# Blocks of 512 tokens in tile order behind one block of 192, in place of 26 blocks of 480

## Chip, core and metric

The kernel runs on one core of a Trainium2 chip. The metric is the device time of one execution in microseconds (us); the time shown is the median of three runs. The core's engines are TensorE (PE in the rows, its weight loads PEld), VectorE (DVE), ScalarE (ACT), GpSimd (POOL) and SyncE (SP, which issues the DMAs).

## What is computed

12480 tokens of 128 channels go through an attention with 32 inducing points and then through two feed-forward layers of width 2048. All inputs are float32 or float64; the output is float32.

```python
def mab(q, kv):
    s = scale * (q @ kv.transpose(0, 2, 1))
    s = s - s.max(-1, keepdims=True)
    a = np.exp(s)
    a /= a.sum(-1, keepdims=True) + 1e-09
    return a @ kv
h = mab(I, x)                                # 32 inducing points attend to all tokens
x = mab(x, h)                                # each token attends to the 32 rows of h
x = (s * np.maximum(x @ w_in, 0)**2 + b) @ w_out                       # layer 1
x = f(x @ w_in2) @ w_out2       # layer 2; f(h) = h if h>=1, 0 if h<=-1, else (h+1)**2/4
```

## The kernel before, in words

**Tiling.** The tokens are cut into `NB` = 26 blocks of `TB` = 480 = `TP` x `KB` = 120 partitions x 4 tokens (lines 21 to 25). A block is loaded with four consecutive tokens on each partition, turned by four TensorE transposes, and copied from PSUM to `xT[bl]` with a strided write that restores the order of the tokens (`transposes`, line 240). For the layers a block is the moving operand of every matmul, 480 columns wide; the inner width 2048 is 16 chunks of 128, two chunks to a step, so a block takes `SPB` = 8 steps and the kernel 208 steps for each layer.

**Attention.** In groups of four blocks: `scores` (each block's 32 rows side by side in one PSUM bank), a running maximum, the exponential, and `weighted`, which sums tokens into `hsum`. `finish` makes `hT`, 128 columns wide. Beside it the float64 weights of both layers are loaded as pairs of 32-bit words and converted to float32 (`convert`, line 369), in 16 pieces of 512 columns; the last pieces are those of layer 2.

**First block.** `first_soft` makes the layer-1 input `qt[0]` of block 0 by a way of its own (`f_st` to `f_qt`, lines 770 to 799). The other blocks go in groups of four through `soft_scores` to `soft_move`, and one by one through `soft_q` and `soft_split`. 26 blocks make groups of 1, 4, 4, 4, 4, 4, 4 and 1.

**A step.** Step t does layer 1 of step t and layer 2 of step t - `LAG`, with `LAG` = 13. Layer 1: `in1` has 2 matmuls on float32r operands, `relu1` and `sq1` run on ScalarE, `split1` on GpSimd, and `out1` has one float32 matmul, which the trace shows as two records, and 3 float32r ones. Layer 2: `in2` has 6 float32r matmuls, `clip2`, `g2` and `split2_lo` run on VectorE, `sq2` on ScalarE, `split2_hi` in turns on ScalarE and GpSimd, `out2` has 6 float32r matmuls, and after 8 steps `store` turns the block and writes it with four DMAs. In all, 17 float32r matmuls and one float32 matmul to a step; all of them take new weights.

**The ramp.** Before step 13 only layer 1 runs (`ramp_step`, line 865), beside the conversions, and its `out1_whole` uses two float32 matmuls to a step. Layer 2 can begin its element-wise work only when `close` has given the conversions' space to it, after the last conversion.

**Order.** Each engine runs its instructions in the order in which they were written out. For the attention, the ramp and the last 13 layer-2 steps, a small planner (`Plan`, line 83) places every operation by modelled costs and the list `JOBS` or `TJOBS`, and `best` takes the engine on which an operation would end first; between them the order within a step is the string `ORDER`.

```python
def in1(t):
    nc.tensor.matmul(p[:, j, :TB], hw[f // 4][:, ...], qt[bl], start=True, stop=True)
def out1(t):
    nc.tensor.matmul(p, wo_w[:, f0, :], g[:, 0, :], start=(f0 == 0), stop=False)      # float32
    nc.tensor.matmul(p, wo_hi[:, f1, :], hi[:, 0, :], start=False, stop=False)        # float32r
```

Of the kernel before, what the change touches and what calls it, by code (L numbers as in the profile page):

```python
# [17 lines left out]
C = 128  # L18
NM = 32
DFF = 2048  # L20
TP = 120
KB = 4
TB = TP * KB
NB = 26
NQ = TB // NM
GB = 4
# [23 lines left out]
T1 = 201  # L50
# [25 lines left out]
i195 i196 h194 u206 u207 v c195 c196 l194 i197 g195 i198 g196 c197 g197 s195 o193 c198 i199 o194  # L76
g198 i200 o195 s196 c199 i201 o196 g199 c200 s198 g200 c201 s197 i202 c202 o197 i203 s200 g202 o198
g201 s199 c203 i204 g203 s201 o199 s202 i205 o200 s203 c204 i206 c205 o201 o202 g205 s205 o203 g204
c206 i207 s204 g206 s206 c207 o204 o205 o206 g207 s207 o207
"""  # L80

# [56 lines left out]
def moe_attn_kernel(ctx: ExitStack, tc: tile.TileContext, x, ind, w_in, w_out, s, b, w_in2, w_out2, out):  # L138
# [10 lines left out]
    xT = [kt([C, TB], f"xT{i}") for i in range(NB)]  # L149
# [71 lines left out]
    def blocks(g):  # L221
        return range(min(GB, NB - g * GB))

    def load_x(g, *deps):
        def one_block(i):
            if i == 0:
                xc[g] = pre.tile([TP, GB * KB, C], F32, tag="xc", name=f"xc{g}", bufs=XB)
            t0 = (g * GB + i) * TB
            nc.sync.dma_start(out=xc[g][:, i * KB:(i + 1) * KB, :],
                              in_=x[0][t0:t0 + TB].rearrange("(p k) c -> p k c", k=KB))  # L230

        for i in blocks(g):
            xd[g, i] = dma(0.69, lambda i=i: one_block(i), *deps, at=g * XPACE)
# [5 lines left out]
    def transposes(g):  # L239
        for i in blocks(g):  # L240
            bl = g * GB + i

            def on_pe(i=i, bl=bl):
                T["tr", bl] = ptile("tr", f"ptr{bl}", TRB)
                for k in range(KB):
                    nc.tensor.transpose(T["tr", bl][:, k * TP:(k + 1) * TP], xc[g][:, i * KB + k, :], ident[:TP, :TP])

            def evac(eng, bl=bl):
# [3 lines left out]
            t = add("PE", 0.8 if g == 0 else 0.41, on_pe, xd[g, i], P.get(("xT", bl - TRB)))  # L252
            P["tr", bl] = t
            P["xT", bl] = best(tuple(c for c in (("ACT", 0.45), ("DVE", 0.57)) if c[0] in EVAC), evac, t)

    def scores(g):
        nb = len(blocks(g))
        n = NM * nb

        def on_pe():  # L260
            ps = T["sc", g] = ptile("sc", f"psc{g}", 2)
            for i in blocks(g):
                nc.tensor.matmul(ps[NM * i:NM * (i + 1), :TB], iT, xT[g * GB + i], start=True, stop=True)

        def top():
            ps, old = T["sc", g], T.get(("m", g - 1))
            m = T["m", g] = small("m", g)
            if g == 0:
                nc.vector.reduce_max(m, ps[:, :TB], axis=AX.X)
            else:  # L270
                mx = small("mx", g)
                nc.vector.reduce_max(mx[:n], ps[:n, :TB], axis=AX.X)
# [6 lines left out]
        def expo():  # L279
# [3 lines left out]
            nc.scalar.activation(e[:n], ps[:n, :TB], AF.Exp, bias=nm[:n], scale=scale, accum_out=l[:n])  # L283
# [8 lines left out]
        xs = [P["xT", g * GB + i] for i in blocks(g)]  # L292
# [6 lines left out]
    def weighted(g):  # L299
        nb = len(blocks(g))  # L300
        n = NM * nb

        def tr():
            pe = T["pe", g] = pp.tile([128, KB, 128], F32, tag="pe", name=f"pe{g}", bufs=1)
            e = T.pop(("e", g))[:n].rearrange("n (p k) -> n k p", k=KB)
            for k in range(KB):
                nc.tensor.transpose(pe[:TP, k, :n], e[:, k, :], ident[:n, :n])

        def evac(eng):
            eT = T["eT", g] = pre.tile([TP, KB, 128], F32, tag="eT", name=f"eT{g}", bufs=3)  # L310
            copy(eng, eT[:, :, :n], T.pop(("pe", g))[:TP, :, :n])

        def on_pe():
            ph, eT = ptile("ph", f"ph{g}", 1), T.pop(("eT", g))
            T["ph", g] = ph
            for k in range(KB):
                for i in blocks(g):
                    nc.tensor.matmul(ph[NM * i:NM * (i + 1), :C], eT[:, k, NM * i:NM * (i + 1)],
                                     xc[g][:, i * KB + k, :], start=(k == 0), stop=(k == KB - 1))
# [191 lines left out]
    def finish():  # L511
        t = add("PE", 0.12, f_pm, P["top", NG - 1], P["xT", NB - 1])
# [106 lines left out]
    def step_tile(tag, t, bufs, dt=F32):  # L619
        p = pool["wk" if tag in ("g1", "hi1", "lo1") else "wk2"]  # L620
        return p.tile([128, 1 if tag in ("hi1", "lo1") else GW, TB], dt, tag=tag, name=f"{tag}_{t}", bufs=bufs)

    def relu1(t):
        g = step_tile("g1", t, G1B)
        nc.scalar.activation(g, h1.pop(t)[:, :, :TB], AF.Relu)  # L625
        g1[t] = g
# [19 lines left out]
    def outp(t, hi, lo, whi, wlo, acc, nm, js=range(GW)):  # L646
# [4 lines left out]
        p = acc[bl][:, :TB]  # L651
# [7 lines left out]
    def y1_of(t):  # L659
# [3 lines left out]
        return y1p[bl][:, :TB]  # L663
# [17 lines left out]
    def evac1(bl):  # L681
        y1f[bl] = wtile([128, TB], "y1f", f"y1f{bl}", 1)
        nc.scalar.activation(y1f[bl], y1p.pop(bl)[:, :TB], AF.Identity, bias=bcol, scale=s_sb)

    def evac1_hi(bl, eng="Pool"):
        y1h[bl] = wtile([128, TB], "y1h", f"y1h{bl}", YB, F32R)
        copy(eng, y1h[bl], y1f[bl])

    def evac1_lo(bl, eng="Pool"):
        y1l[bl] = wtile([128, TB], "y1l", f"y1l{bl}", YB, F32R)  # L690
# [5 lines left out]
    def in2(t, js=range(GW)):  # L696
# [42 lines left out]
    def store(bl):  # L739
        o = pool["wk2"].tile([128, NQ, NM], F32, tag="o", name=f"o{bl}", bufs=2)  # L740
# [29 lines left out]
    def f_st():  # L770
        ps = T["st"] = mbank("st_0")
        for k in range(KB):
            nc.tensor.matmul(ps[:TP, 0, k * NM:(k + 1) * NM], xT[0].rearrange("c (p k) -> c k p", k=KB)[:, k, :],
                             hT[:, :NM], start=True, stop=True)

    def f_se():
        e = sm[0, "e"] = wtile([128, NQ, NM], "se", "se0")[:TP, :KB, :]
        nc.vector.tensor_copy(e, T.pop("st")[:TP, 0, :KB * NM].rearrange("p (k j) -> p k j", j=NM))
# [3 lines left out]
    def f_sd():  # L782
        soft_sum(0)
        soft_mul(0, "DVE")
        a2 = T["a2"] = wtile([TP, KB, 2, 2, NM], "qin", "a2", GB)
        eb = sm[0, "e"].unsqueeze(2).to_broadcast([TP, KB, 2, NM])
# [3 lines left out]
    def f_sq():  # L790
        ps = T["qt"] = bank("qt_0")
        for k in range(KB):
            nc.tensor.transpose(ps[:, 0, k * TP:(k + 1) * TP],
                                T["a2"][:, k].rearrange("p h r j -> p (h r j)"), ident[:TP, :TP])

    def f_qt():
        q = qt[0] = wtile([128, TB], "qt", "qt0", 2, F32R)
        nc.vector.tensor_copy(q.rearrange("c (p k) -> c k p", k=KB),
                              T.pop("qt")[:, 0, :TB].rearrange("c (k p) -> c k p", k=KB))
# [6 lines left out]
    def first_soft():  # L806
        t = P["st"] = add("PE", 0.42, f_st, P["hT"])
        t = add("DVE", 0.6, f_se, t)
        left["h2"].append(t)
        t = add("ACT", 0.21, lambda: soft_e(0), t)  # L810
# [314 lines left out]
```

## Time and profile before

| | |
|---|---|
| time, median of 3 runs | 1056.59 us (1055.17 to 1060.0) |
| the profiled execution's own time | 1055.07 us |
| its span, first to last instruction | 1053.3 us |
| PE busy | 1014.7 us, 96% of the span |
| DVE busy | 841.9 us, 80% |
| ACT busy | 787.3 us, 75% |
| POOL busy | 664.2 us, 63% |

A row of the timeline gives start, time taken, engine, line, operation, the tile written and those read, shapes, and in square brackets the idle time before it and what ended it. Matmuls overlap, so the cost of one in a dense stretch is the distance from its start to the next one's start, not its duration. In the table of stretches, each engine's busy time stands with its number of instructions, and PEclk is TensorE's granted clock as a share of 2.4 GHz.

### The profile page before, as it was taken

What the parts mean: (1) busy time and instruction counts of PE and PEld (TensorE: products, weight loads), DVE (VectorE), ACT (ScalarE), POOL (GpSimd) and SP (SyncE); (2) the same over time, 40 slices, a digit from 0 to 9 for tenths busy, and PEclk for the clock granted to TensorE, in tenths of its full rate; (3) what the DMA queues carried; (4) which work ended last, traced back from release to release, by engine and by line L of the source; (5) the groups of instructions that cost most, each with busy time, mean ns of one, the idle gap of its engine ahead of it and who ended that gap; (6) DMA issues with size and microseconds to landing.
All of it is one profiled execution on the core that took longest, in us unless ns stands there. A gap on an engine that the chain in (4) does not pass through costs nothing.

```text
span 1053.3 us, 12315 instructions
## 1 busy us (share of the span) xinstructions
PE 1014.7 (96%) x4445; PEld 777.8 (74%) x4445; DVE 841.9 (80%) x850; ACT 787.3 (75%) x842; POOL 664.2 (63%) x680
## 2 busy tenths in 40 slices
PE   6886899999999999999999999999999999999997
PEld 4553577777777777777777777777777777777775
DVE  4899978877887778788777887877887778877776
ACT  6747478778787777787777777777877777877754
POOL 3757657665567656576656666565766656665565
PEclk9988899999999999999999999999999999999999
DMA  8712001100001000011000010000020000000001
GB/s 260 225 43 76 1 0 27 31 7 4 10 10 38 10 10 10 1 19 38 1 10 10 10 33 15 10 8 3 13 44 1 10 10 10 10 11 10 0 10 20
DMA packets 65668, 28.13 MB, mean 27 GB/s; under 512 B 54135, under 2 KB 61463, under 8 KB 65607
## 3 DMA queue, kind: packets, MB, share of 16 engines
q1 hardware_dynamic: 65606, 27.35, 11.3%
q8 instruction: 35, 0.57, 0.2%
q14 instruction: 27, 0.21, 0.1%
HBM read 14.80 MB, written 6.39 MB: 20 GB/s over the span
## 4 chain that ended last, share of the span: by engine, by line
PE 87%; DVE 7%; ACT 1%; issue 1%; POOL 1%; SPq 0%; DMA 0%; DVEq 0%; ACTq 0%; POOLq 0%
PE y L669 15%; PE y L655 8%; PE y L656 8%; PE h L704 8%; PE y L657 8%; PE h L706 8%; PE h L705 8%; PE h L615 8%; PE y L671 4%; PE y L672 4%; PE y L670 4%; DVE cva_out L404 1%; PE s L550 1%; DVE cva_out L408 1%; DVE cvs_out L401 0%
## 5 line engine op out<-in xcount | busy, mean ns | idle before, releaser
L711 DVE TENSOR_SCALAR cl<-h 128x960 f32<-128x960 f32 (+1 forms) x210 | 239.7, 1143 | 106.8 <-PE h L706 105.4
L182 POOL TENSOR_SCALAR hi<-g 128x480 fp32r<-128x480 f32 x195 | 132.9, 682 | 298.4 <-PE y L672 294.9
L625 ACT ACTIVATE g<-h 128x960 f32<-128x960 f32 x208 | 202.4, 973 | 146.2 <-PE h L615 141.3
L733 DVE TENSOR_TENSOR lo<-oo,hi 128x960 fp32r<-128x960 f32 x196 | 243.7, 1243 | 69.0 <-ACT hi L178 54.8
L715 ACT ACTIVATE cl<-cl,mhalf 128x960 f32<-128x960 f32 (+1 forms) x210 | 228.5, 1090 | 73.0 <-DVE cl L711 73.0
L640 POOL TENSOR_TENSOR lo<-g,hi 128x480 fp32r<-128x480 f32 x195 | 240.3, 1232 | 16.3
L720 DVE SCALAR_TENSOR_TENSOR oo<-h,cl 128x960 f32<-128x960 f32 (+1 forms) x210 | 238.0, 1136 | 7.8 <-ACT cl L715 4.4
L630 ACT ACTIVATE g<-g 128x960 f32<-128x960 f32 x206 | 207.5, 1008 | 5.7
L669 PE MATMUL y<-g,wo_w 128*128 128x480 f32 x390 | 188.6, 565 | 0.0
L704 PE MATMUL h<-y1h,wi_hi 128*128 128x480 f32 x416 | 159.3, 383 | 5.0 <-DVE oo L720 5.0
L655 PE MATMUL y<-hi,wo_hi 128*128 128x480 f32 x416 | 159.3, 383 | 0.6 <-ACT hi L178 0.6
L706 PE MATMUL h<-y1l,wi_hi 128*128 128x480 f32 x416 | 159.0, 382 | 0.0
L705 PE MATMUL h<-y1h,wi_lo 128*128 128x480 f32 x416 | 158.8, 382 | 0.0
L657 PE MATMUL y<-hi,wo_lo 128*128 128x480 f32 x416 | 158.0, 380 | 0.0
L656 PE MATMUL y<-lo,wo_hi 128*128 128x480 f32 x402 | 153.7, 382 | 0.8 <-DVE lo L733 0.7
L670 PE MATMUL y<-hi,wo_hi 128*128 128x480 f32 x195 | 146.6, 752 | 0.6 <-POOL hi L182 0.6
L615 PE MATMUL h<-qt,hw 128*128 128x480 f32 x416 | 127.4, 389 | 1.8 <-ACT g L625 1.1
L178 ACT CAST hi<-oo 128x960 fp32r<-128x960 f32 (+1 forms) x110 | 105.9, 966 | 3.8 <-DVE oo L720 2.1
L182 POOL TENSOR_SCALAR hi<-oo 128x960 fp32r<-128x960 f32 x100 | 100.6, 1006 | 2.9 <-DVE oo L720 2.9
L655 PEld LDWEIGHTS y<-hi,wo_hi 128*128 128x128 f32 x416 | 78.2, 188 | 19.0 <-POOL lo L640 4.7
L615 PEld LDWEIGHTS h<-qt,hw 128*128 128x128 f32 x416 | 78.3, 189 | 18.8 <-issue 2.5
L704 PEld LDWEIGHTS h<-y1h,wi_hi 128*128 128x128 f32 x416 | 78.2, 188 | 18.4 <-DVE oo L720 3.7
(146 smaller groups left out, 1216.4 us busy)
## 6 DMA issues: line engine op xcount, KB each, us to landing
xc<-in_x_dram SPq DMA_DIRECT2D x26, 240.0 KB, 6.1
out_dram<-o SPq DMA_DIRECT2D x104, 60.0 KB, 2.0
qin<-se SPq DMA_DIRECT2D x100, 60.0 KB, 2.0
raw_in<-in_moe_w_in_dram SPq DMA_DIRECT2D x8, 512.0 KB, 6.0
raw_out<-in_moe_w_out_dram SPq DMA_DIRECT2D x8, 512.0 KB, 6.1
ind_sb<-in_inducing_dram SPq DMA_DIRECT2D x1, 16.0 KB, 6.5
s_sb<-in_moe_s_dram SPq DMA_DIRECT2D x1, 0.5 KB, 6.2
b_sb<-in_moe_b_dram SPq DMA_DIRECT2D x1, 0.5 KB, 6.0
```

Source lines behind the costliest of these rows:

```text
L615: nc.tensor.matmul(p[:, j, :TB], hw[f // 4][:, (f % 4) * 128:(f % 4 + 1) * 128], qt[bl], start=True, stop=True)
L640: engine[eng].tensor_sub(lo1[t], g1[t][:, 1:], hi1[t].bitcast(F32))
L655: nc.tensor.matmul(p, whi[:, f, :], hi[:, j, :], start=first, stop=False)
L656: nc.tensor.matmul(p, whi[:, f, :], lo[:, j, :], start=False, stop=False)
L657: nc.tensor.matmul(p, wlo[:, f, :], hi[:, j, :], start=False, stop=last)
L669: nc.tensor.matmul(p, wo_w[:, f0, :], g[:, 0, :], start=(f0 == 0), stop=False)
L704: nc.tensor.matmul(p[:, j, :TB], wi2_hi[:, fs], y1h[bl], start=True, stop=False)
L705: nc.tensor.matmul(p[:, j, :TB], wi2_lo[:, fs], y1h[bl], start=False, stop=False)
L706: nc.tensor.matmul(p[:, j, :TB], wi2_hi[:, fs], y1l[bl], start=False, stop=True)
L711: nc.vector.tensor_scalar(cl[t][:, part(js)], h2[t][:, part(js), :TB], -1.0, 1.0, op0=ALU.max, op1=ALU.min)
L720: nc.vector.scalar_tensor_tensor(oo[t][:, part(js)], h2[t][:, part(js), :TB], -1.0, cl[t][:, part(js)], op0=ALU.max, op1=ALU.add)
L733: engine[eng].tensor_sub(lo2[t][:, part(js)], oo[t][:, part(js)], hi2[t][:, part(js)].bitcast(F32))
```

## The change

Blocks have 512 tokens (128 partitions x 4), and there are 25: block 0 has 192 tokens (96 partitions x 2), the other 24 have 512. Every matmul, element-wise operation and tile of a block takes its width from `tb(bl)`. The tokens of a block stay in the order of its tiles (column k x 128 + p is the token on partition p, place k) from the transposes to the output; `store` puts the order right in the address pattern of its DMAs. The copies out of PSUM in `transposes` and `f_qt`, and the reads of `e` in `weighted`, are contiguous thereby. The attention takes blocks 1 to 24 in six groups of four and block 0 last by itself. There are 200 steps in place of 208, `LAG` stays 13, the end's list `TJOBS` is the same list with every number 8 lower, and the groups of the second attention are 1 and six times 4. The planner's costs of ScalarE, VectorE and GpSimd operations are scaled with the block (`us`). The diff, cut to its core:

```diff
-TP = 120
+TP = 128
 KB = 4
 TB = TP * KB
-NB = 26
+TP0, KB0 = 96, 2
+TB0 = TP0 * KB0
+NB = 25
...
-T1 = 201
+T1 = 193
...
+def tokens(bl):
+    if bl:
+        return TP, KB, TB, TB0 + (bl - 1) * TB
+    return TP0, KB0, TB0, 0
+def tb(bl):
+    return TB if bl else TB0
+def us(d, bl):
+    return 0.06 + (d - 0.06) * tb(bl) / 480
...
     def blocks(g):
-        return range(min(GB, NB - g * GB))
+        return list(enumerate(range(g * GB + 1, (g + 1) * GB + 1) if g < NG - 1 else [0]))
...
             def evac(eng, bl=bl, n=n):
-                copy(eng, xT[bl].rearrange("c (p k) -> c k p", k=KB),
-                     T.pop(("tr", bl))[:, :TB].rearrange("c (k p) -> c k p", k=KB))
+                copy(eng, xT[bl], T.pop(("tr", bl))[:, :n])
...
-            nc.tensor.matmul(p[:, j, :TB], hw[f // 4][:, (f % 4) * 128:(f % 4 + 1) * 128], qt[bl],
+            nc.tensor.matmul(p[:, j, :tb(bl)], hw[f // 4][:, (f % 4) * 128:(f % 4 + 1) * 128], qt[bl],
                              start=True, stop=True)
...
-        p = acc[bl][:, :TB]
+        p = acc[bl][:, :tb(bl)]
...
-        nc.vector.transpose(o.rearrange("p q d -> p (q d)"), y2p.pop(bl)[:, :TB])
-        ov = out[bl * TB:(bl + 1) * TB].rearrange("(q t) (r d) -> r t q d", t=NM, d=NM)
+        nc.vector.transpose(o.rearrange("p q d -> p (q d)"), y2p.pop(bl)[:, :n])
+        ov = out[t0:t0 + n].rearrange("(q t k) (r d) -> r t k q d", t=NM, k=kb, d=NM)
         for r in range(C // NM):
-            nc.sync.dma_start(out=ov[r], in_=o[NM * r:NM * (r + 1)])
+            nc.sync.dma_start(out=ov[r], in_=o[NM * r:NM * (r + 1)].rearrange("p (k q) d -> p k q d", k=kb))
...
-        for k in range(KB):
-            nc.tensor.matmul(ps[:TP, 0, k * NM:(k + 1) * NM], xT[0].rearrange("c (p k) -> c k p", k=KB)[:, k, :],
+        for k in range(KB0):
+            nc.tensor.matmul(ps[:TP0, 0, k * NM:(k + 1) * NM], xT[0][:, k * TP0:(k + 1) * TP0],
                              hT[:, :NM], start=True, stop=True)
...
-        a2 = T["a2"] = wtile([TP, KB, 2, 2, NM], "qin", "a2", GB)
+        a2 = T["a2"] = wtile([TP0, KB0, 2, 2, NM], "qin", "a2", GB)
...
-        nc.vector.tensor_copy(q.rearrange("c (p k) -> c k p", k=KB),
-                              T.pop("qt")[:, 0, :TB].rearrange("c (k p) -> c k p", k=KB))
+        nc.vector.tensor_copy(q, T.pop("qt")[:, 0, :TB0])
...
-        sq = best((("ACT", 0.89), ("DVE", 1.07), ("Pool", 2.17)), lambda e: sq1(a, e), t, bias=SQB)
+        sq = best((("ACT", us(0.95, bl)), ("DVE", us(1.07, bl)), ("Pool", us(2.17, bl))), lambda e: sq1(a, e), t, bias=SQB)
```

## Rows read from the trace of the kernel before

**Rows 1.** Table of stretches: start and end, length, busy times, clock, DMA, GB/s.
```profile
60.00:70.00 10.00, 7.81 (x23) 4.49 (x23) 9.07 (x16) 1.70 (x4) 7.26 (x8) 0.67 0.20 52
...
100.00:110.00 10.00, 6.08 (x10) 2.83 (x11) 9.86 (x12) 0.46 (x1) 7.40 (x6) 0.59 0.00 0
...
120.00:130.00 10.00, 6.72 (x21) 5.43 (x20) 9.20 (x9) 6.87 (x7) 5.38 (x5) 0.66 0.01 2
...
200.00:400.00 200.00, 200.00 (x846) 157.17 (x845) 158.87 (x148) 156.38 (x162) 126.59 (x135) 1.00 0.07 13
...
600.00:800.00 200.00, 200.00 (x845) 157.16 (x844) 160.66 (x152) 156.87 (x163) 128.73 (x135) 1.00 0.09 18
```

**Rows 2.** Chain that ended last, in order of time (start, us, what): steady steps.
```profile
146.46 0.81 PE y L669 x2
150.98 0.81 PE y L669 x2
...
868.43 0.92 PE s L550 x2
```

**Rows 3.** Timeline of PE at full clock, 703 to 705 us.
```profile
703.12 0.38 PE L704 MATMUL h<-y1h,wi_hi 128*128 128x480 f32 x1
...
704.88 0.38 PE L657 MATMUL y<-hi,wo_lo 128*128 128x480 f32 x1
```

**Rows 4.** Timeline of PE at half clock, 126 to 127 us.
```profile
126.11 0.60 PE L655 MATMUL y<-hi,wo_hi 128*128 128x480 f32 x1
126.51 0.60 PE L656 MATMUL y<-lo,wo_hi 128*128 128x480 f32 x1
```

**Rows 5.** Timeline of PEld: weight loads for matmuls of one column.
```profile
63.87 0.86 PEld L843 LDWEIGHTS bsum<-b_sb,wo_s 128*128 128x128 f32 x7 [0.40 <-issue]
```

**Rows 6.** Timeline of DVE in the ramp.
```profile
62.35 0.96 DVE L575 TENSOR_SCALAR mx<-mx 120x4 f32<-120x4 f32 x1
...
63.55 1.22 DVE L580 TENSOR_TENSOR se<-se,mx 120x128 f32<-120x128 f32 x1
64.80 0.67 DVE L787 CAST a<-se 120x256 fp32r<-120x256 f32 x1
65.51 1.45 DVE L788 TENSOR_TENSOR a<-se,a 120x256 f32<-120x256 f32 x1
...
68.00 1.01 DVE L798 CAST qt<-qt 128x480 fp32r<-128x480 f32 x1 [0.33 <-PE qt L793]
...
71.58 1.16 DVE L632 TENSOR_TENSOR g<-g 128x960 f32<-128x960 f32 x1 [0.44 <-ACT g L625]
...
101.65 2.22 DVE L632 TENSOR_TENSOR g<-g 128x960 f32<-128x960 f32 x1
```

**Rows 7.** ACT's copies out of PSUM, grouped by form.
```profile
L178 ACT COPY xT<-ptr 128x480 f32<-128x480 f32 x26 | 25.1, 1095 | 8.0 <-PE ptr L246 8.0
...
L178 ACT COPY eT<-pe 120x512 f32<-120x512 f32 x6 | 3.9, 654 | 0.0
```

**Rows 8.** Timeline of all engines, 13 to 18 us.
```profile
13.71 3.66 ACT L178 COPY xT<-ptr 128x480 f32<-128x480 f32 x4 [2.89 <-PE ptr L246]
...
17.84 0.43 DVE L401 TENSOR_SCALAR cvs_in<-cvs_in 128x512 f32<-128x512 f32 x1 [4.28 <-ACT cvs_in L387]
```

**Rows 9.** Chain that ended last, where layer 2 begins.
```profile
118.48 1.57 DVE wo_lo L427
120.04 1.08 DVE cl L711
...
121.20 1.10 ACT cl L715
...
122.33 1.17 DVE oo L720
...
123.54 0.77 PE h L704
```

**Rows 10.** Chain that ended last, near the end.
```profile
1020.52 2.26 POOL lo L733
...
1041.73 1.17 DVE lo L733
```

More of the change, by code (lines that the diff above doesn't have):

```diff
@@ L20 @@
 DFF = 2048
-TP = 120
+TP = 128
 KB = 4
 TB = TP * KB
-NB = 26
+TP0, KB0 = 96, 2
+TB0 = TP0 * KB0
+NB = 25
 NQ = TB // NM
+NQ0 = TB0 // NM
 GB = 4
@@ L148, in moe_attn_kernel @@
     ident = kt([128, 128], "ident")
-    xT = [kt([C, TB], f"xT{i}") for i in range(NB)]
+    xT = [kt([C, tb(i)], f"xT{i}") for i in range(NB)]
     wo_w = kt([128, WH, C], "wo_w")
@@ L221, in blocks, with one_block @@
     def blocks(g):
-        return range(min(GB, NB - g * GB))
+        return list(enumerate(range(g * GB + 1, (g + 1) * GB + 1) if g < NG - 1 else [0]))
     def load_x(g, *deps):
-        def one_block(i):
+        def one_block(i, bl):
             if i == 0:
                 xc[g] = pre.tile([TP, GB * KB, C], F32, tag="xc", name=f"xc{g}", bufs=XB)
[L228 to L233, printed above, removed]
+            tp, kb, n, t0 = tokens(bl)
+            nc.sync.dma_start(out=xc[g][:tp, i * KB:i * KB + kb, :],
+                              in_=x[0][t0:t0 + n].rearrange("(p k) c -> p k c", k=kb))
+        for i, bl in blocks(g):
+            xd[g, i] = dma(us(0.69, bl), lambda i=i, bl=bl: one_block(i, bl), *deps, at=g * XPACE)
     def dma(dur, fn, *deps, at=0.0):
@@ L258, in scores @@
         n = NM * nb
+        cols = tb(blocks(g)[0][1])
         def on_pe():
             ps = T["sc", g] = ptile("sc", f"psc{g}", 2)
-            for i in blocks(g):
-                nc.tensor.matmul(ps[NM * i:NM * (i + 1), :TB], iT, xT[g * GB + i], start=True, stop=True)
+            for i, bl in blocks(g):
+                nc.tensor.matmul(ps[NM * i:NM * (i + 1), :cols], iT, xT[bl], start=True, stop=True)
         def top():
@@ L290, in total @@
                                            op0=ALU.mult, op1=ALU.add)
-        xs = [P["xT", g * GB + i] for i in blocks(g)]
+        xs = [P["xT", bl] for _, bl in blocks(g)]
         P["sc", g] = add("PE", 0.22 * nb, on_pe, *xs, P["iT"], P.get(("ex", g - 2)), P.get(("sc", g - 1)))
@@ L301, in weighted @@
         n = NM * nb
+        tp, kb, _, _ = tokens(blocks(g)[0][1])
         def tr():
             pe = T["pe", g] = pp.tile([128, KB, 128], F32, tag="pe", name=f"pe{g}", bufs=1)
-            e = T.pop(("e", g))[:n].rearrange("n (p k) -> n k p", k=KB)
-            for k in range(KB):
-                nc.tensor.transpose(pe[:TP, k, :n], e[:, k, :], ident[:n, :n])
+            e = T.pop(("e", g))
+            for k in range(kb):
+                nc.tensor.transpose(pe[:tp, k, :n], e[:n, k * tp:(k + 1) * tp], ident[:n, :n])
         def evac(eng):
             eT = T["eT", g] = pre.tile([TP, KB, 128], F32, tag="eT", name=f"eT{g}", bufs=3)
-            copy(eng, eT[:, :, :n], T.pop(("pe", g))[:TP, :, :n])
+            copy(eng, eT[:tp, :kb, :n], T.pop(("pe", g))[:tp, :kb, :n])
         def on_pe():
@@ L315, in on_pe @@
             T["ph", g] = ph
[L316 to L319, printed above, removed]
+            for k in range(kb):
+                for i, _ in blocks(g):
+                    nc.tensor.matmul(ph[NM * i:NM * (i + 1), :C], eT[:tp, k, NM * i:NM * (i + 1)],
+                                     xc[g][:tp, i * KB + k, :], start=(k == 0), stop=(k == kb - 1))
         def total():
```

121 lines of the change are left out of this document (62 added, 59 removed).

## Prediction

> **What bounds the kernel now.** I read the table of stretches first. From 130 us to near the end TensorE has no idle time at all and the full clock, while VectorE and ScalarE are busy for about 80% [rows 1]: there the time is the sum of the matmuls. Before 130 us it is otherwise. VectorE is busy for 91 to 99% of the ramp's stretches while TensorE waits, partly at half clock [rows 1]; the chain of waits runs along VectorE's conversions of weights up to 120.04 us, and only then layer 2 starts [rows 9]. So the change has two accounts: what TensorE must still do after the ramp, and when the ramp ends.
>
> Next, the price of a matmul. In the chain a step starts every 4.52 us, and its float32 matmul (two records) takes 0.81 us [rows 2]; the other 17, float32r, take (4.52 - 0.81) / 17 = 0.218 us. The timeline agrees: eight distances in 1.76 us are 0.220 us each [rows 3]. At 2.4 columns per ns 480 columns are 0.200 us, so about 0.018 us are over. At half clock the distance is 0.40 us, which is 480 columns at 1.2 GHz with nothing over [rows 4]. The float32 matmul passes its columns four times, 0.800 us at full clock, with 0.01 over. What the 0.018 us are decides this change, and since every float32r matmul after the ramp has 480 columns the trace can't show it directly:
> - a fixed cost of each matmul: 512 columns take 0.2133 + 0.018 = 0.2313 us;
> - a lower rate for float32r: 0.218 x 512 / 480 = 0.2325 us;
> - a floor that the columns don't set: 0.218 us still (a rival, below).
> Weight loads in front of matmuls of one column follow each other at (0.86 - 0.19) / 6 = 0.112 us [rows 5] (0.19 us is the duration of a single load), so a load alone is no floor of 0.218 us. I take 0.232 us, between the first two, which differ little.
>
> The Trainium skill, page "TensorE: Matmul & The Clock Gate", section "Back-to-back issue gap", gives a warm distance of N / 2.4 + 2.5 ns, so 202.5 ns for 480 columns and 215.8 ns for 512. The trace disagrees: 218 ns at 480. If the excess over that rule were only a floor, its 215.8 ns would fit below 218 ns, and the sum would be that of the floor rival.
>
> **The matmuls after the ramp.** Before: layer 1 has 208 - 13 = 195 steps with 2 + 3 float32r matmuls and one float32; layer 2 has 208 steps with 12. That is 975 + 2496 = 3471 float32r x 0.218 + 195 x 0.81 = 756.7 + 158.0 = 914.7 us. After: layer 1 has 200 - 13 = 187 steps, all at 512 columns; layer 2 has 192 steps at 512 and 8 at 192. That is 935 + 2304 = 3239 x 0.232 = 751.4 us; 96 narrow matmuls; 187 x 0.81 x 512 / 480 = 187 x 0.864 = 161.6 us. A narrow matmul streams for 0.08 us, less than a weight load, so I take the load's 0.112 us [rows 5], 10.8 us in all; its bounds are 0.098 us (0.08 + 0.018) and 0.324 us (the float32 matmul's 0.81 x 192 / 480). The sum is 923.8 us: +9.1 us. It grows although 128 matmuls fewer run in 8 steps fewer, because 13 steps of the ramp now cover 8 x 192 + 5 x 512 = 4096 token-steps of layer 1 in place of 13 x 480 = 6240. The 2144 missing ones come later. A step of 512 takes 17 x 0.232 + 0.864 = 4.81 us; 4.52 x 512 / 480 is 4.82 us: wider blocks alone bring next to nothing. With 0.2313 us the sum is 2.3 us less, with 0.2325 us 1.6 us more.
>
> **The ramp.** What is gained must come here, and VectorE sets its end, so I count VectorE's work.
> - First block's softmax: the sum's TENSOR_SCALAR, the multiplication, the two steps of `a2` and the copy to `qt` take 0.96 + 1.22 + 0.67 + 1.45 + 1.01 = 5.31 us [rows 6]. The last four halve or better (128 and 256 elements to a partition become 64 and 128; the copy goes from 480 to 192 and is now contiguous); the 0.96 us were spent on four elements and may stay. I take -2.4 us (-1 to -3.5).
> - Squares of layer 1 that the planner gave to VectorE: 1.16 and 2.22 us [rows 6]. The first is of block 0 and falls to about 0.5 us; the second, of block 1, grows to 2.36 us or goes to ScalarE, which block 0's narrow steps leave freer. I take -1.5 us (+0.1 to -3.4).
> - `xT` copies: strided, 1095 ns; a contiguous copy of 512 columns from PSUM is 654 ns [rows 7]. That frees ScalarE some 24 x 0.44 = 10 us, but ScalarE sets no end later. It matters at 13.7 us, where four copies run for 3.66 us and VectorE waits 4.28 us for the square queued behind them [rows 8]. Four times about 0.35 us is 1.4 us; I take -1.3 us (0 to -1.4, zero if a DMA was the later one).
> - The attention's last group, 192 columns in place of 480: one maximum and one exponential shorter, -0.6 us. The output part of layer 1 for block 0 is smaller, -0.35 us; the groups of the second attention are wider, +0.3 us.
> Together -5.9 us, from +1 to -9 with the order of the queues left open: a planner places all of it anew, and the same conversions on VectorE take twice as long in some places as in others.
>
> At layer 2's start `clip2`, `sq2` and `g2` of the first step run one after another from 120.04 to 123.50 us before TensorE goes on [rows 9]. With 384 in place of 960 elements they take about half: -1.8 us (0 to -2).
>
> **The rest.** One group of the second attention is gone: -0.9 us, its matmuls in the chain [rows 2]. At the end, between 1017 and 1043 us, the chain passes 14 operations of VectorE, ScalarE and GpSimd, 13.7 us in all, such as 2.26 and 1.17 us [rows 10]; 6.7% more columns make +0.9 us. The store's DMAs move the same bytes in as many pieces of 128 bytes, beside other work but for the last: 0, at most +0.5 us. In the steady steps all engines' operations grow with TensorE's step, so none becomes the bound: 0. In the eight narrow steps TensorE has 5 x 0.232 + 0.864 + 12 x 0.112 = 3.37 us, and ScalarE, which in a full step has 156.38 / 200 of 4.81 us [rows 1], 3.76 us, has less than that with layer 2 narrow: 0, at most +0.4 us to a step, 3 us.
>
> **The sum.** +9.1 - 5.9 - 1.8 - 0.9 + 0.9 = +1.4 us. The profiled execution took 1055.1 us (a span of 1053.3 us and 1.8 us around it), so it would be 1056.5 us; it lies 1.5 us below the median, so by the median 1058 us. With the bounds of each term the forecast reaches from 1050 to 1065 us.
>
> **Rivals.**
> - *The float32r distance is a floor.* If weight load and hand-over make the 0.218 us, 512 columns (0.2133 us) fit under it. Then 3335 x 0.218 + 161.6 = 888.6 us, 26.1 us less than now; with the other terms (-7.7 us) the median is 1023 us. For it: the half-clock distance has nothing over [rows 4], as under a floor. Against: loads alone come every 0.112 us [rows 5]. Chance 0.10.
> - *Columns and weights share a read rate.* 480 + 128 columns in 0.218 us are 2789 per us; 512 + 128 take 0.2295 us, and the narrow ones 0.115 us. The matmuls come to 916.0 us, +1.3 us, and the median to 1050 us. The lack of any excess at half clock and in float32 fits this too. Chance 0.12.
> - *The ramp gives more:* every VectorE term at its good end, the median at 1050 to 1052 us. Chance 0.10.
> - *The narrow block is dear (slower).* Place: steps 13 to 20, 96 matmuls of layer 2. If they cost 0.218 us each, that is +10.2 us, 1068 us; at the float32 price of 0.324 us +20.4 us, 1078 us. It decides from about 0.16 us on, where it adds 4 us to the forecast. For it: no float32r matmul of under 480 columns is in the trace. Against: one-column matmuls run at the load's 0.112 us [rows 5]. Chance 0.15.
> - *The ramp doesn't shrink:* VectorE's conversions only fill the freed time with waits for GpSimd. Then the matmuls' +9.1 us stay, less a little: 1064 us. Chance 0.08.
>
> **How the numbers follow.** The forecast has 0.45. A measurement of this kernel tells about 0.5%, 5.3 us, from no change, so "same" is 1051.3 to 1061.9 us. Faster: the floor 0.10, the shared rate 0.10 of 0.12, the larger ramp gain 0.08 of 0.10, and 0.04 of the forecast: 0.32. Slower: 0.12 of the narrow block, 0.07 of the ramp that doesn't shrink and 0.09 of the forecast: 0.28. The rest, 0.40, is the same. The range 1043 to 1069 us leaves out the floor (0.10) and the dearer half of the narrow block (0.07).
>
> **What would show it.** In the profile after: the distance of float32r matmuls at 512 columns (0.231 to 0.233 us forecast, 0.218 us floor, 0.2295 us shared) and a step of 4.81 us; that of the narrow ones in layer 2's first eight steps (0.112 us); the last conversion's end on VectorE about 6 us before 120 us and TensorE going on 1.7 us after it; TensorE without idle time between. I am wrong most if the distance at 512 columns is near 0.218 us or that at 192 columns is not near 0.11 us.

## The result, and the profile after

The changed kernel takes 1065.7 us (median of 5 runs, 1065.04 to 1066.77) against 1056.59 us: ratio 1.008, interval 1.0057 to 1.0103. It is slower by 9 us, 0.7 us beyond the upper end of the forecast (1065 us), though inside the range. The profiled execution took 1066.77 us with a span of 1065.0 us; that of the kernel before had 1053.3 us.

The table of stretches after, with the columns of [rows 1]:

```profile
60.00:70.00 10.00, 6.96 (x34) 5.90 (x34) 8.94 (x19) 2.65 (x5) 8.12 (x8) 0.80 0.17 53
...
100.00:110.00 10.00, 4.63 (x8) 1.89 (x7) 9.83 (x12) 5.92 (x7) 6.50 (x6) 0.75 0.00 0
...
120.00:130.00 10.00, 8.36 (x37) 6.16 (x36) 7.50 (x13) 7.70 (x11) 6.72 (x6) 0.83 0.01 2
...
200.00:400.00 200.00, 200.00 (x793) 147.28 (x791) 158.24 (x140) 154.36 (x152) 123.74 (x125) 1.00 0.07 12
```

The picture is the old one: from 140 us to about 1030 us TensorE has no idle time and the full clock; from 60 to 120 us VectorE is busy for 87 to 98% of every 10 us while TensorE waits. So the two accounts of the prediction can be read separately. The chain of waits gives the point where they meet (start, us, what):

```profile
121.81 0.48 DVE cl L734
...
122.31 0.62 ACT cl L738
...
122.95 0.57 DVE oo L743
```

and TensorE's timeline shows where it goes on:

```profile
123.57 0.36 PE L727 MATMUL h<-y1h,wi_hi 128*128 128x192 f32 x1 [1.53 <-DVE oo L743]
```

The last conversion ends at 121.81 us, 1.8 us later than before [rows 9] instead of 6 us earlier. `clip2`, `sq2` and `g2` then take 1.71 us to the end of `oo` in place of 3.46 us, and TensorE goes on at 123.57 us, against 123.54 us before [rows 9]. So in this execution the ramp brought nothing at all. From there to the end of the span it is 1065.0 - 123.57 = 941.4 us in place of 1053.3 - 123.54 = 929.8 us: +11.7 us, where the prediction had +9.1 us.

The matmuls behind that, on TensorE's timeline, first wide, then narrow ones (compare [rows 3]):

```profile
702.80 0.39 PE L728 MATMUL h<-y1h,wi_lo 128*128 128x512 f32 x1
...
705.14 0.40 PE L680 MATMUL y<-hi,wo_lo 128*128 128x512 f32 x1
```

```profile
139.40 0.27 PE L728 MATMUL h<-y1h,wi_lo 128*128 128x192 f32 x1
...
140.51 0.27 PE L680 MATMUL y<-hi,wo_lo 128*128 128x192 f32 x1
```

Ten wide distances in 2.34 us are 0.234 us each (0.2334 us is the mean over the dense part), ten narrow ones in 1.11 us are 0.111 us each. A steady step takes 4.82 us, which is 4.52 x 512 / 480; without its 17 x 0.2334 us, 0.85 us are left for the float32 matmul.

In the ramp VectorE has more squares of layer 1 than before. The operations of that line in both kernels (duration in ns: smallest, median, largest; first and last start; forms), before and after:

```profile
L632 DVE TENSOR_TENSOR g<-g x2: 1159/1688/2217, 71.6 to 101.6; 128x960 f32<-128x960 f32 x2
```

```profile
L655 DVE TENSOR_TENSOR g<-g x5: 999/1390/2282, 74.3 to 103.5; 128x384 f32<-128x384 f32 x4, 128x1024 f32<-128x1024 f32 x1
```

And what TensorE waited for between 60 and 124 us (total us, times, longest), after:

```profile
PE y L702 <- DVE g L655: 13.7, 3, 6.6
PE qt L817 <- DVE a L812: 3.0, 1, 3.0
```

The planner gave VectorE five squares (7.4 us) in place of two (3.4 us). The narrow ones have 384 columns and take 1.0 to 1.6 us, about as long as the smaller of the two with 960 columns (1.16 us), and `out1_whole` stands 13.7 us behind three of the five. The timeline shows what the narrow ones wait for:

```profile
88.44 1.37 POOL L437 TENSOR_TENSOR cvl_out<-cvl_out,cvs_out 128x512 f32<-128x512 f32 x1 [0.37 <-DVE cvs_out L434]
88.62 1.61 DVE L655 TENSOR_TENSOR g<-g 128x384 f32<-128x384 f32 x1
```

Each of the four begins while a GpSimd operation is under way and ends 0.41 us after that operation's end (here 90.23 against 89.82 us), whether it took 1.0 or 1.6 us.

### The profile page after: what moved, and what is told of

The parts are those of the page before. It is cut to its first block, busy times and chain, and to the rows that moved or that the text cites. A ratio compares the mean times of both kernels' runs of the same rounds, so it can differ in the third digit from the quotient of the medians.

```text
span 1065.0 us, 11873 instructions
## 1 busy us (share of the span) xinstructions
PE 1020.1 (96%) x4285; PEld 748.9 (70%) x4285; DVE 834.6 (78%) x821; ACT 769.1 (72%) x807; POOL 667.9 (63%) x656
## 4 chain that ended last, share of the span: by engine, by line
PE 88%; DVE 7%; ACT 1%; issue 1%; POOL 1%; DVEq 0%; ACTq 0%; POOLq 0%
PE y L692 15%; PE y L679 9%; PE y L678 8%; PE y L680 8%; PE h L729 8%; PE h L728 8%; PE h L727 8%; PE h L637 8%; PE y L695 4%; PE y L694 4%; PE y L693 4%; DVE g L655 1%; DVE cva_out L426 1%; PE s L572 0%; DVE cva_out L430 0%
## 5 line engine op out<-in xcount | busy, mean ns | idle before, releaser
L734 DVE TENSOR_SCALAR cl<-h 128x1024 f32<-128x1024 f32 (+2 forms) x202 | 238.7, 1184 | 121.0 <-PE h L729 121.0
L648 ACT ACTIVATE g<-h 128x1024 f32<-128x1024 f32 (+1 forms) x200 | 200.8, 1004 | 158.3 <-PE h L637 155.9
L756 DVE TENSOR_TENSOR lo<-oo,hi 128x1024 fp32r<-128x1024 f32 (+1 forms) x188 | 238.4, 1268 | 69.1 <-ACT hi L197 54.8
L738 ACT ACTIVATE cl<-cl,mhalf 128x1024 f32<-128x1024 f32 (+2 forms) x202 | 226.0, 1121 | 67.5 <-DVE cl L734 67.5
L663 POOL TENSOR_TENSOR lo<-g,hi 128x512 fp32r<-128x512 f32 x187 | 242.3, 1296 | 15.6
L743 DVE SCALAR_TENSOR_TENSOR oo<-h,cl 128x1024 f32<-128x1024 f32 (+2 forms) x202 | 237.2, 1176 | 8.6 <-ACT cl L738 5.1
L653 ACT ACTIVATE g<-g 128x1024 f32<-128x1024 f32 (+1 forms) x195 | 205.0, 1051 | 5.4
L692 PE MATMUL y<-g,wo_w 128*128 128x512 f32 x374 | 191.0, 591 | 0.0
L678 PE MATMUL y<-hi,wo_hi 128*128 128x512 f32 (+1 forms) x400 | 157.5, 394 | 0.6 <-ACT hi L197 0.6
L729 PE MATMUL h<-y1l,wi_hi 128*128 128x512 f32 (+1 forms) x400 | 156.7, 392 | 0.0
```

What stands on the lines that cost most here:

```text
L663: engine[eng].tensor_sub(lo1[t], g1[t][:, 1:], hi1[t].bitcast(F32))
L678: nc.tensor.matmul(p, whi[:, f, :], hi[:, j, :], start=first, stop=False)
L729: nc.tensor.matmul(p[:, j, :tb(bl)], wi2_hi[:, fs], y1l[bl], start=False, stop=True)
L756: engine[eng].tensor_sub(lo2[t][:, part(js)], oo[t][:, part(js)], hi2[t][:, part(js)].bitcast(F32))
```

## Experiments

Three theories stood against each other: (1) the narrow first block moves layer-1 work out of the ramp, where it was hidden, to where TensorE is the bound; (2) the ramp fails to shrink because the planner puts squares on VectorE; (3) the attention ends later, at a lower clock. In the table, "goes on" is the end of the ramp in the profiled execution, and "from there" the rest of its span. The ratio is to the kernel before, run beside it on the same chip.

| kernel | median us | ratio, interval | `hT` at | goes on | from there |
|---|---|---|---|---|---|
| before | 1056.59 | | 58.30 | 123.54 | 929.8 |
| after | 1065.7 | 1.0057 to 1.0103 | 62.56 | 123.57 | 941.4 |
| after, once more | 1065.57 (1 run) | | 59.99 | 120.86 | 942.8 |
| eight widths | 1004.88 (1 run) | | 60.20 | 121.08 | |
| strided copies | 1067.51 | 1.0097 to 1.0127 | 61.60 | 123.57 | 942.1 |
| zeros in the attention | 1065.41 | 1.0078 to 1.0112 | 60.11 | 121.13 | 941.3 |
| 16 ramp steps | 1070.31 | 1.0127 to 1.0158 | 61.57 | 132.3 | 937.6 |
| no squares on VectorE | 1062.45 | 1.0044 to 1.0083 | 62.37 | 120.19 | 941.9 |
| the same, with zeros | 1061.6 | 1.0035 to 1.0072 | 59.69 | 117.49 | 941.9 |
| before, no squares on VectorE | 1054.75 | 0.9979 to 1.0004 | 59.90 | 123.84 | 930.1 |
| narrow block last | 1062.09 | 1.0047 to 1.0074 | 61.23 | 132.28 | 927.6 |
| narrow last, no squares on VectorE | 1053.49 | 0.9970 to 0.9987 | 61.02 | 124.29 | 928.1 |
| no zeros at the attention's end | 1065.58 | 1.0077 to 1.0105 | 60.41 | 121.42 | 941.4 |
| narrow last, no squares, no zeros | 1053.99 | 0.9975 to 0.9994 | 60.88 | 123.53 | 928.1 |

**What sets a float32r matmul's distance.** The second of `in2`'s three matmuls, of `out2`'s and of `out1`'s float32r ones get widths that change with the step, so part of the products is left out.

```diff
+def width(t, n):
+    return min(n, (512, 480, 448, 384, 320, 256, 192, 128)[t % 8])
...
-            nc.tensor.matmul(p[:, j, :tb(bl)], wi2_lo[:, fs], y1h[bl], start=False, stop=False)
+            m = width(t, tb(bl))
+            nc.tensor.matmul(p[:, j, :m], wi2_lo[:, fs], y1h[bl][:, :m], start=False, stop=False)
```

> The changed kernel with one of the three float32r matmuls of each group (the second of in2, of out2 and of out1's float32r ones) cut to 512, 480, 448, 384, 320, 256, 192 or 128 columns, by the step's place in its block; so part of the products is left out of the sums. Distance from such a matmul to the next one. If float32r streams at a lower rate (0.219 us for 480, 0.233 for 512, so 0.456 ns a column): 0.204 at 448, 0.175 at 384, 0.146 at 320, 0.117 at 256, and the weight load's 0.112 at 192 and 128. If each matmul has a fixed cost of 0.019 us on top of 2.4 columns per ns: 0.206 at 448, 0.179 at 384, 0.152 at 320, 0.126 at 256, 0.112 at 192 and 128. If columns and the next weights share one read rate: 0.187 at 384, 0.163 at 320, 0.140 at 256, 0.117 at 192. The recorded durations should fall by 0.456 ns a column under the first and 0.417 ns under the second.

Matmuls of one line, grouped by shape (count | busy us, mean ns of one | idle):

```profile
L735 PE MATMUL h<-y1h,wi_lo 128*128 128x512 f32 x48 | 19.0, 396 | 0.0
...
L735 PE MATMUL h<-y1h,wi_lo 128*128 128x480 f32 x48 | 18.2, 379 | 0.0
...
L735 PE MATMUL h<-y1h,wi_lo 128*128 128x384 f32 x48 | 16.2, 338 | 0.0
...
L735 PE MATMUL h<-y1h,wi_lo 128*128 128x256 f32 x48 | 13.4, 279 | 0.0
```

The duration is a distance plus a constant pipeline, so its slope is the distance's: (396 - 279) / 256 = 0.457 ns per column, and 512 x 0.457 = 234 ns leaves no fixed cost. Float32r passes 2.19 columns per ns at the full clock, at every width from 256 to 512. What happens below that shows on the timeline:

```profile
500.83 0.22 PE L735 MATMUL h<-y1h,wi_lo 128*128 128x128 f32 x1
500.89 0.45 PE L736 MATMUL h<-y1l,wi_hi 128*128 128x512 f32 x1
501.18 0.39 PE L733 MATMUL h<-y1h,wi_hi 128*128 128x512 f32 x1
...
501.99 0.28 PE L684 MATMUL y<-lo,wo_hi 128*128 128x256 f32 x1
502.11 0.39 PE L685 MATMUL y<-hi,wo_lo 128*128 128x512 f32 x1
502.34 0.40 PE L682 MATMUL y<-hi,wo_hi 128*128 128x512 f32 x1
```

A 128-column matmul is followed after 0.06 us, but the one after that comes only 0.29 us later, in place of 0.23 us. The two distances together are 0.06 us more than their columns need, which is about what 128 columns leave uncovered of a weight load of 0.11 us [rows 5]. At 256 columns (0.12 us) nothing is paid. So the lower rate is right, the fixed cost, the floor and the shared rate fall, and wider blocks can't make float32r cheaper per token.

**Strided copies of `xT` again.** Theory 3: contiguous copies let TensorE run ahead in the attention and then wait (3.70 us at 28 us, for an exponential), at half clock.

```diff
-                copy(eng, xT[bl], T.pop(("tr", bl))[:, :n])
+                copy(eng, xT[bl].rearrange("c (p k) -> c k p", k=4), T.pop(("tr", bl))[:, :n].rearrange("c (p k) -> c k p", k=4))
```

> The changed kernel with ScalarE's copies of xT out of PSUM made in strides of four columns again (same values, same places), which cost 1095 ns each before. Theory: the contiguous copies let TensorE run ahead of VectorE in the attention, it then waits 3.7 us in one piece, its clock falls to half, and hT comes at 62.6 us in place of 58.3. Then the strided copies fill that wait again: full clock from 20 to 50 us, hT near 59 us, the last conversion 2 to 4 us earlier than 121.8 us, time 1062 to 1064 us. Rival: the copies have nothing to do with the clock; the attention is as late or later for ScalarE's extra 10 us, time 1065 to 1070 us.

The clock is full from 20 to 50 us, where the first profile of the changed kernel has 0.66 and 0.68 from 30 to 50 us. But `hT` comes only 1 us earlier, TensorE goes on at the same 123.57 us, and the time is 2 us higher, inside the rival's range. That the copies set the clock isn't shown either: the same kernel once more (below) has the contiguous copies and 0.97, 0.86 and 0.83 in these three stretches. What the run does show is the price of the strided copies: 1.8 us by the medians, so the contiguous ones are worth about that.

**Zeros to keep TensorE at work.** 3, 14 and 6 matmuls on zeros ahead of the transposes of the exponential in groups 1, 2 and 4.

```diff
             e = T.pop(("e", g))
+            n_idle = {1: 3, 2: 14, 4: 6}.get(g, 0)
...
+                for _ in range(n_idle):
+                    nc.tensor.matmul(t[:, :IW], wz[:, :128], wz[:, :IW], start=True, stop=True)
```

> The changed kernel with matmuls on zeros (3, 14 and 6 of 128 columns) put on TensorE's queue ahead of the transposes of e of the groups 1, 2 and 4, where it waited 0.9, 3.7 and 1.5 us. Theory: TensorE's half clock from 30 to 37 and 44 to 50 us makes the attention late. Then the granted clock stays at 1.00 there, hT comes 3 to 4 us earlier, and the time is 1062 to 1064 us. Rival: VectorE's queue sets the attention's pace whatever TensorE's clock is: hT within 1 us of 62.6 us and the time 1065 to 1067 us.

`hT` came 2.4 us earlier and so did the ramp's end, in the profiled execution; the median fell by 0.3 us, within what can't be told apart. The next run gives a reason.

**The changed kernel once more.**

> The changed kernel once more, unchanged, for how far its ramp varies from one execution to another. If the ramp's loss is fixed in the order of its instructions: hT at 62.6 us and the last conversion's end at 121.8 us, each within 0.5 us. If it hangs on chance of the start (DMAs, clock): one of them is off by 1 us or more, as in the kernel with the eight widths, whose attention is the same (60.2 and 119.3 us).

The second answer: without any edit, `hT` is at 59.99 us and TensorE goes on at 120.86 us, 2.7 us earlier than in the first profile. The ramp varies by that much from one execution to another: in the five profiles whose attention is the same (these two, the eight widths, the 16 ramp steps and the one without squares on VectorE) `hT` is at 59.99, 60.20, 61.57, 62.37 and 62.56 us. So theory 3 rested on a profile at the late end of that spread. The two executions part early. These are the transposes of four blocks on TensorE, the first time and once more:

```profile
12.12 3.65 PE L266 MATMUL ptr<-ident,xc 128*128 128x128 f32 x16 [0.88 <-DMA xc<-in_x_dram]
```

```profile
11.19 2.53 PE L266 MATMUL ptr<-ident,xc 128*128 128x128 f32 x16
```

VectorE's first conversion behind them starts at 17.01 and at 15.06 us, which is 1.95 of the 2.6 us by which `hT` differs. The span gained only 1.3 us of it (1063.7 against 1065.0 us), because after the ramp the granted clock stayed at half for 6.8 us in place of 3.4 us. So the ramp's end and the rest of the span aren't quite independent, and for the ramp only medians, or differences well over 3 us, can be read below.

**No zeros at the attention's end.** In the first profile of after the chain to `hT` passes matmuls on zeros that the planner lays into TensorE's gaps. There are 16 records of them (the kernel before has 2, off the chain), which are 8 matmuls, since the 23 added above show as 46 records:

```profile
57.60 1.49 PE idle L1016 x6
59.09 0.99 PE ph L340 x4
60.09 2.01 PE idle L1016 x8
```

```diff
-    for t in plan.gaps("PE", P["ex", NG - 2][1], P["hT"][0], cost, IDLE):
-        add("PE", cost, on_idle0, P["ex", NG - 2], at=t)
```

> The changed kernel without the 16 matmuls on zeros that the planner lays into TensorE's gaps at the attention's end; they stand on the chain to hT with 1.49 + 2.01 + 0.43 us, where the kernel before has 2 of them and none on the chain. Theory (they are on the path to hT): hT is written 3 to 4 us earlier than in the changed kernel (at 56 to 59.5 us; 62.6 and 60.0 us with them), the last conversion ends 1 to 3 us earlier (at 117 to 120 us), and the time falls to 1062 to 1065 us. Rival (they only fill a wait, or the clock falls without them and takes the time back): hT at 60 to 62.6 us still, and a time of 1065 to 1067 us. Second rival (hT isn't what the conversions wait for): hT earlier, but the conversions' end and the time as they were.

The rival is right: 1065.58 us. The chain at the same place without the zeros:

```profile
55.98 0.33 DVE cvs_out L434
56.31 0.60 DVE cva_in L426
56.91 1.41 DVE cvs_out L423
58.31 0.26 DVE hsum L348
...
58.60 0.93 DVE hsum L543
```

`hsum` now waits for conversions ahead of it in VectorE's queue, and `hT` is at 60.41 us, inside the spread that it has with the zeros. A long piece on the chain was the cover of another wait.

**More steps in the ramp.** Theory 1 says that a longer lead of layer 1 should give back what the narrow block took.

```diff
-LAG = 13
+LAG = 16
+TAIL = 13
...
-KP = 4
+KP = 2
...
-a8 a9 c14 q2 a10 c15 a11 a12
+a8 a9 c14 q2 a10 c15 a11 a12 a13 a14 a15
```

> The changed kernel with LAG = 16 in place of 13: sixteen layer-1 steps in the ramp (8 of 192 and 8 of 512 tokens, 5632 token-steps in place of 4096; the kernel before had 6240), and the planner for 2 in place of 4 steps after it. Theory: the changed kernel is slower mainly because layer-1 work has moved out of the ramp, where TensorE has idle time, to where it has none; then three steps of 5 x 0.233 + 0.86 = 2.03 us leave the dense part, 6.1 us, and the time is 1059 to 1061 us with the conversions' end unchanged. Rival: the ramp has no room for them (their whole out1 is 1.7 us each on TensorE, after a square that VectorE makes late), layer 2 starts 4 to 6 us later and the time stays at 1064 to 1067 us.

From where TensorE goes on, 937.6 us are left in place of 941.4 us, as theory 1 wants in kind; but the ramp has no room for the three steps. The chain from one of the last squares on VectorE:

```profile
117.13 2.21 DVE g L656
...
119.38 5.40 PE y L703 x8
124.78 0.47 PE h L638 x2
...
125.28 1.03 ACT g L649
```

The `out1_whole` of two steps (four float32 matmuls, eight records) had been held up behind that square and run only after it. The last conversion ends at 121.52 us, as before, but layer 2's element-wise work starts at 130.5 us, later than the rival had it, and the time rises to 1070.31 us.

**VectorE barred from the squares of the ramp.**

```diff
-        sq = best((("ACT", us(0.95, bl)), ("DVE", us(1.07, bl)), ("Pool", us(2.17, bl))), ...)
+        sq = best((("ACT", us(0.95, bl)), ("Pool", us(2.17, bl))), ...)
```

> The changed kernel, with VectorE barred from the squares of layer 1 in the ramp (the planner may choose ScalarE or GpSimd only); nothing else differs. Theory (the ramp's loss is work that the planner put on VectorE, 5 squares of 7.4 us where 2 of 3.4 us stood before): the last conversion ends 4 to 7 us before 121.8 us, TensorE goes on at 117 to 119 us, and the time falls from 1065.7 to 1059 to 1062 us. Rival (VectorE's conversions fill the freed time with waits for GpSimd or for weights): the last conversion ends within 1 us of 121.8 us and the time stays 1064 to 1067 us. Second rival (the squares only move to an engine that is as late): layer 1's output waits for ScalarE or GpSimd, and the time is above 1067 us although the conversions end earlier.

1062.45 us: 3.2 us less by the medians, just short of what theory 2 expected. Its runs, 1061.55 to 1063.82 us, lie below all of the changed kernel's, the one beside it on the same chip (1065.57 us) included, though the intervals of the two ratios overlap. The conversions end at 118.42 us. Taking 7.4 us away from VectorE gave back less than half. The chain shows what is late next:

```profile
111.50 1.32 POOL qt L620
...
112.89 1.33 POOL cvl_out L437
...
114.30 1.60 POOL cvl_out L442
...
115.92 0.85 DVE wo_hi L199
...
116.79 1.63 DVE wo_lo L449
```

The last piece waits for GpSimd, which first finishes the split of a later block's `qt`.

> The same, and 23 matmuls on zeros ahead of the transposes of the exponential in three groups of the attention, which keep TensorE at work while it would wait. Theory (squares and attention each cost their part, and the parts add): hT is written at about 60 us, the last conversion ends 2 us before that of the kernel without the zeros, and the time is 1 to 2.5 us lower than its. Rival (the attention's end is hidden behind the conversions): hT earlier, conversions and time within 0.5 us of it.

Zeros in the attention on top of it: 0.85 us less by the medians, between the theory (1 us or more) and the rival (0.5 us or less), so this run decides nothing; its ramp ends earliest of all (117.49 us).

> The kernel before (26 blocks of 480), with VectorE barred from layer 1's squares in the ramp in the same way: 2 squares of 3.4 us move. Theory: the last conversion ends 2 to 3 us before 120.0 us, and the time falls by 2 to 3 us, to 1053 to 1055 us; so what the squares cost is no matter of the block's width. Rival: no change, 1056 us.

In the kernel before, the same edit changes nothing that can be told (1054.75 us, interval 0.9979 to 1.0004); the ramp's end doesn't move (123.84 us). There TensorE's longest wait becomes GpSimd's `hi`, 6.5 us. So two squares on VectorE cost nothing that can be told, five did: VectorE's busy time isn't paid one for one.

**The narrow block last.** This undoes one part of the change, the place of the narrow block, and keeps the width of the rest.

```diff
 def tokens(bl):
-    if bl:
-        return TP, KB, TB, TB0 + (bl - 1) * TB
-    return TP0, KB0, TB0, 0
+    if bl < NB - 1:
+        return TP, KB, TB, bl * TB
+    return TP0, KB0, TB0, bl * TB
 def tb(bl):
-    return TB if bl else TB0
+    return TB if bl < NB - 1 else TB0
...
+    sizes = [1] + [GB] * ((NB - 1) // GB - 1) + [GB - 1, 1]
```

> The changed kernel with the narrow block of 192 tokens last instead of first: 24 blocks of 512, then 192; groups of the second attention 1, 4, 4, 4, 4, 4, 3, 1; the rest as it is. The 13 steps of the ramp then cover 13 x 512 = 6656 token-steps of layer 1 in place of 4096. Theory (what TensorE has left after the ramp is what the narrow first block put there): by the same prices (0.2334, 0.864, 0.112 us) the matmuls after the ramp are 9 us fewer, so from where TensorE goes on to the end 929 to 933 us in place of 941.4 us; the ramp has a wide first block again, so TensorE goes on at 122 to 126 us, and the time is 1053 to 1058 us, level with 26 blocks of 480. Rival (wide blocks themselves cost): 938 to 942 us from there on, and a time of 1063 us or more. Second rival (the ramp can't take 13 wide steps, as it couldn't take 16): TensorE goes on after 128 us, and the time is above 1060 us.

```profile
132.28 0.80 PE L726 MATMUL h<-y1h,wi_hi 128*128 128x512 f32 x1 [3.82 <-DVE oo L742]
```

Theory 1's main number came, and went beyond its range: from where TensorE goes on it takes 927.6 us, 13.8 us less than in the changed kernel. Not all of it is the 9 us of the matmuls: with a narrow block last, TensorE's waits in the last layer-2 steps fall from 3.8 to 1.2 us, and what follows its last matmul from 5.8 to 5.1 us. The second rival came with it: the ramp ends at 132.28 us, and the time is 1062.09 us. What TensorE waited for from 60 to 132 us in this kernel:

```profile
PE y L701 <- DVE g L654: 10.4, 4, 8.5
PE qt L816 <- DVE a L811: 3.5, 1, 3.5
```

Five squares of 1024 columns are on VectorE here, and one of them holds TensorE for 8.5 us. Barring them:

> The same, with VectorE barred from layer 1's squares in the ramp. Theory (the squares cost here what they cost behind a narrow first block): 1 to 3 us below the kernel with the narrow block last. Rival (as with blocks of 480, where barring them brought nothing that can be told): within 1 us of it.

1053.49 us, 8.6 us less; the theory had the sign and at most about a third of the size. The five squares were 6.3 us of VectorE's time, so here more came back than was taken away. TensorE goes on 8 us earlier:

```profile
124.29 0.80 PE L726 MATMUL h<-y1h,wi_hi 128*128 128x512 f32 x1 [2.90 <-DVE oo L742]
```

So the ramp does take 13 wide steps. This kernel is faster than the one before by 0.2% (0.9970 to 0.9987). Its last conversions:

```profile
112.11 0.43 DVE L199 CAST wi_hi<-cvl_in 128x512 fp32r<-128x512 f32 x1 [2.56 <-POOL cvl_in L442]
...
118.16 0.83 DVE L199 CAST wo_hi<-cvl_out 128x512 fp32r<-128x512 f32 x1 [2.79 <-POOL cvl_out L442]
```

VectorE is idle twice for over 2.5 us here, both times until GpSimd is done: the end of the ramp is now the way of two pieces through VectorE and GpSimd in turn, not VectorE's work alone.

> The narrow block last, VectorE barred from layer 1's squares in the ramp, and no zeros at the attention's end. Theory (each part costs for itself): 1 to 3 us less than with the first two alone, so 1050.5 to 1052.5 us, 3 to 5 us below 26 blocks of 480. Rival (the conversions' end is set by the way of each piece through VectorE and GpSimd and not by hT): 1053 to 1054 us.

1053.99 us: the rival. The zeros don't count here. What an earlier `hT` would bring isn't shown, since it stayed where it was (60.88 and 61.02 us).

## Why the prediction was right and wrong

**Right: where the time is bound, and that wide blocks bring nothing by themselves.** A step of 4.81 us was forecast and 4.82 us measured, the narrow matmul at 0.112 us came at 0.111 us, layer 2's start was to gain 1.8 us and gained 1.75 us. The narrow block as a *dear* block fell. The argument that 2144 token-steps move behind the ramp held, and the experiments confirm it: with the narrow block last, 13.8 us are gone behind the ramp's end, some 3 us of them at the tail.

**Mis-sized: the matmuls after the ramp,** +9.1 us forecast, +11.7 us measured (11.5 to 13.0 us over all kernels with the narrow block first and 13 ramp steps, against 929.8 us). The value taken was 0.232 us, between a fixed cost and a lower rate; the runs show the lower rate alone, 0.2334 us. With 4.82 in place of 4.808 us a step, 187 steps make 2.2 us, most of what was missing. The bound from the lower rate (+1.6 us) was nearly that. The tail's +0.9 us came: TensorE's waits in the last layer-2 steps and what follows its last matmul are 8.7 us before and 9.6 us after. The gain of 0.9 us for one soft group wasn't measured alone.

By the rule N / 2.4 + 2.5 ns, which the Trainium skill ("TensorE: Matmul & The Clock Gate", section "Back-to-back issue gap") gives for the isolated gap of a single matmul, 512 columns would take 215.8 ns; the runs show 233.4 ns, and a slope instead of an offset. The measurement decides: for float32r the rule's 2.4 columns per ns is not reached.

**Wrong: the ramp, -5.9 us.** This step turned the forecast from slower to no change. It added up VectorE's operations as if each microsecond taken from them came off the ramp's end. The runs show otherwise: taking 3.4 us of squares away changed nothing in the kernel before, 7.4 us gave 3.2 us with the narrow block first, 6.3 us gave 8.6 us with it last. The sizes were off too. Term by term, with the rows of [rows 6 to 8]:
- The squares were to give 1.5 us, with +0.1 us as the worst bound, and VectorE spent 4.0 us more on them (7.4 against 3.4 us; 6.8 us in the repetition). The prediction treated the two squares as fixed work that shrinks with the block; it is a choice of the planner, made anew. Why it chose five isn't shown: with the narrow block last it chose five as well, all of 1024 columns, so narrow operations that look cheap aren't needed for it. The edit also raised ScalarE's modelled cost of a square from 0.89 to 0.95 us at 480 columns and left VectorE's at 1.07 us; no run took that back. The planner's cost doesn't hold the wait for GpSimd that made the narrow ones 1.0 to 1.6 us long.
- The first softmax was to give 2.4 us. Its five operations now take 0.99 + 0.52 + 1.32 + 0.75 + 0.34 = 3.92 us in place of 5.31 us: -1.4 us. The copy to `a2` even doubled, from 0.67 to 1.32 us for half the elements:

```profile
65.49 0.99 DVE L597 TENSOR_SCALAR mx<-mx 96x2 f32<-96x2 f32 x1
...
66.71 0.52 DVE L602 TENSOR_TENSOR se<-se,mx 96x64 f32<-96x64 f32 x1
67.26 1.32 DVE L811 CAST a<-se 96x128 fp32r<-96x128 f32 x1
```

- The `xT` copies fell from 0.9 to 0.58 us, as said, but in the first profile the conversion behind them starts only 0.8 us earlier and its wait grew from 4.28 us [rows 8] to 4.78 us:

```profile
17.01 0.43 DVE L423 TENSOR_SCALAR cvs_in<-cvs_in 128x512 f32<-128x512 f32 x1 [4.78 <-ACT cvs_in L409]
```

In the repetition it starts 2.8 us earlier, and the strided copies cost 1.8 us of time, so this term (-1.3 us) was about right.

With the first profile's sizes and the two small terms as forecast (-0.95 and +0.3 us) the sum is +4.0 - 1.4 - 0.8 - 0.65 = +1.15 us; with the repetition's it is +3.5 - 1.4 - 2.8 - 0.65 = -1.35 us. The last conversion's end moved by +1.8 us and by -0.9 us (119.10 us). So the sums come near, but the two small terms were not measured, and the runs without squares say that such a sum isn't paid one for one. The term that failed by most is the squares. Theory 2 is shown by two pairs of runs, clearly with the narrow block last (8.6 us), less so with it first (3.2 us), theory 1 by what follows the ramp in all kernels; theory 3 found no support in the medians.

That the measured time lies inside the range is luck in part: the forecast's own bounds ended at 1065 us, and the range went on to 1069 us for a narrow block dearer than its weight loads, which it wasn't. Two small readings of the prediction were off and moved nothing: VectorE is busy for 87 to 99% of the stretches from 60 to 130 us, not 91 to 99%, and 136 float32r and 8 float32 matmuls are gone, not 128.

The rival that conversions fill the freed time with waits for GpSimd (0.08, 1064 us) came nearest the outcome, for another reason: freed time wasn't offered until the squares were gone; then the waits for GpSimd did appear. What stays open is why the planner put five squares on VectorE. That a square on VectorE waits for the GpSimd operation under way is read from the rows above; no run took GpSimd's work away.

## What to carry to other kernels

Where one engine is the bound from some point on, count what a new tiling moves across that point: 2144 token-steps that had been hidden cost more than every gain at the edges. An edit to blocks and costs under a planner can change where all work goes; a term for "the same work, smaller" needs the plan made anew, or a bound that lets the work move the wrong way. And profile the same kernel twice before explaining a start-up stretch: here it moved by 2.7 us by itself, and a cause read from one execution (a late attention) was then not confirmed by three experiments.

## What the hardware showed that was not expected

- Float32r matmuls pass 2.19 columns per ns at the full clock (0.457 ns each, 256 to 512 columns) with no fixed cost, while at half clock 480 columns took 0.40 us, 1.2 columns per ns [rows 4]. The float32 matmul beside them doesn't show the lower rate: its 0.85 us are 4 x 512 columns at 2.4 per ns.
- A matmul shorter than the weight load delays the one behind it, not itself: 0.06 us after 128 columns, then 0.29 us for 512.
- VectorE's squares of 384 columns took 1.0 to 1.6 us in the ramp, each ending 0.41 us after the GpSimd operation that was under way when it began; four of 1024 columns in the kernel with the narrow block last, none begun under a GpSimd operation, took 1.21 to 1.22 us. There the operation's width says less about its time than what GpSimd is doing.
